# A planned attention and mixture-of-experts kernel: constant products in TensorE's waits, a new order of the first loads, a new list of keys

## The chip, the core and the metric

The kernel runs on one core of one Trainium2 chip. TensorE (PE), VectorE (DVE), ScalarE (ACT), GpSimd (POOL) and SyncE (SP) each work through a queue of their own in program order and meet at semaphores. The metric is the device time of one execution in microseconds, median of three runs: 529.28 us (529.21 to 529.37).

## The reference

Attention over 4 batches of 8 heads (768 positions, head size 64), where a query sees the first 4 keys and the 128 keys up to itself. The result, as 3072 rows of 512, goes to the one of 8 experts whose normalised embedding has the largest dot product with the row, weighted by the softmax over the 8.

```python
scores = scale * q @ k.T
keep = is_sink | in_window
a = exp(where(keep, scores, -1e9) - max); a /= sum
x = (a @ v) as [3072, 512]
logits = (x/|x|) @ (emb/|emb|).T / tau
e = argmax(logits); gate = softmax(logits)[e]
out[rows of e] = gate * (relu(x @ w1[e]) @ w2[e])
```

## The kernel before

The attention works on 16 pairs of heads (`p`), each in 6 blocks of 128 queries (`n = 6 p + j`), in two groups of three blocks. For a block: scores on PE into one of three `sp` buffers (`scores`, L1134), the mask and the maximum on DVE (`merge` L1142 to L1146, `top` L1152), the exponential on ACT (`exp`, L1163), which frees the `sp` buffer. For a group: transposes on PE (L1229), copied out by ACT to `PT` (L1234), cut to the window by POOL to `PA` (L1313 to L1317); the four sink columns go by POOL (`psn`, L1213 to L1219), PE (L1286) and ACT (`pst`, L1291); then the values on PE (`av`, L1328 and L1331), a copy on ACT (`oT`, L1336), and products with the identity and the expert embeddings (`xe`, L1341), whose result `xr` goes to DRAM rows `xs`, and whose logits are summed.

Pairs 0 and 1 are "plain": their keys and queries are used as fp32 from `raw1` and `raw2` (`early_loads` loads them, L1072 scales the queries). Later pairs are split into two fp32r parts: keys `kn` to `kt` by ACT (`k1`, L1096) and POOL (`k2`, L1099), queries `qn` on DVE (L1103, L1107).

After every fourth pair the batch is routed (`route`): argmax on DVE, rank products on PE (L399 to L403), places and one-hots on DVE, `bv` on POOL (L431), the table products on PE (L437), which give `perm`, the list of rows for each expert. The last batch is routed in two halves; there ACT also makes the counts `cnt` (L1407 to L1409), and PE reads the first expert's width from them.

The order on all queues is written by a planner (`Plan.order`): every task has an engine, a duration, a key and dependencies; a simulated clock takes, of the tasks that could start within 0.1 us of the earliest, the one with the lowest key. Keys are block numbers plus the offsets in `KEYS` (for the last pair `LAST`). The SP queue carries most loads; eight DMAs can be under way, so the ninth load waits for the first issued, the tenth for the second.

Then comes one section with its own order (`moe`): POOL gathers the rows of the first expert by `perm`; PE runs three products of 512 columns with constants (L628), reads the widths, and branches (`Switch`) to one of 17 copies ("arms") of an expert's PE code, by width. A hint can announce a branch's target ahead of it; for the first arm `first_width` gives it (L1414), within the attention's plan. In the arm, PE transposes the gathered rows (L646) and runs L691 (first layer) and L730 (second layer).

Of the kernel before, what the change touches and what calls it, by code (L numbers as in the profile page):

```python
# [40 lines left out]
LAST = dict(sel=10.5, ps=35.75, pse=1.25, av=20, ote=-47.25, xe=-20, xee=-8.25, k1=-19, k2=29.25, q1=-74, q2=27.5, sc=4.75, mg=86, tp=-21.5, ex=32.5, sk1=29.75, tr=-21.5, te=64.5, rt=9.75, vs=-1.5, em=23.75, rc=123, lgm=29.75)  # L41
# [3 lines left out]
class Task:  # L45


    def __init__(self, eng, dur, key, fn, deps, use, form):
        self.eng, self.dur, self.key, self.fn, self.deps, self.use, self.form = eng, dur, key, fn, deps, use, form
        self.start = self.end = None  # L50
# [7 lines left out]
class Plan:  # L58
# [7 lines left out]
        "SP": dict.fromkeys(("PE", "ACT", "DVE", "POOL", "SP"), 2.2),  # L66
# [8 lines left out]
    def add(self, eng, dur, key, fn, deps=(), use=(), form=None):  # L75
        t = Task(eng, dur, key, fn, [d for d in deps if d is not None], [b for b in use if b is not None], form)
        for b in t.use:
            b.users.append(t)
        self.tasks.append(t)
        return t  # L80
# [17 lines left out]
    def order(self):  # L98
        todo = {}
        for i, t in enumerate(self.tasks):  # L100
            t.i, t.waits, t.ready, t.next = i, len(t.deps), 0.0, []
# [125 lines left out]
class Kernel:  # L227
# [6 lines left out]
    def constants(self, cp):  # L234
# [8 lines left out]
        raw = self.raw  # L243
        rf = T("rf", [P, 4])
        sv = T("sv", [P, 2])
# [4 lines left out]
        fl = T("fl", [P, 2])  # L250
        nc.vector.tensor_scalar(fl[:, 0:1], sv[:, 0:1], 4.0, None, op0=ALU.is_equal)
        nc.vector.scalar_tensor_tensor(out=fl[:, 1:2], in0=sv[:, 1:2], scalar=128.0, in1=fl[:, 0:1], op0=ALU.is_equal, op1=ALU.mult)
        fi = T("fi", [P, 1], I32)
        nc.vector.tensor_copy(fi[:], fl[:, 1:2])
# [4 lines left out]
        nc.gpsimd.affine_select(out=self.ident[:], in_=one[:], pattern=[[-1, P]], compare_op=ALU.is_equal, fill=0.0, base=0, channel_multiplier=1)  # L259

# [107 lines left out]
    def route(self, b, lg, rp, ps_tile, a=0, m=NB, last=False):  # L368
# [81 lines left out]
        return [("DVE", 1.1, argmax), ("PE", 0.2, rank), ("DVE", 0.4, place), ("DVE", 0.4, index), ("DVE", 0.3, onehot), ("POOL", 0.1 + 0.07 * m, values), ("DVE", 0.07 + 0.134 * m, ranks), ("DVE", 0.3, sums), ("DVE", 0.25, positions), ("PE", 0.4, table), ("DVE", 0.15, gather)]  # L450
# [161 lines left out]
    def head(self, flow):  # L612
# [19 lines left out]

        warm(CAP, 3)
# [407 lines left out]

    def wt(self):
        return self.psw.tile([P, 512], F32, tag="w", name="w")
# [15 lines left out]

    def plain_load(self, p, i, engines=None):  # L1060
# [5 lines left out]
    def prep_plain(self, plan, p):  # L1066
# [5 lines left out]
        t = plan.add("DVE", 0.47, NB * (p - 1) + 1, lambda: self.nc.vector.tensor_scalar(q, q, 0.125, None, op0=ALU.mult), [l], [b])  # L1072
# [43 lines left out]
    def scores(self, n):  # L1116
# [3 lines left out]
        sp = self.pss.tile([P, 2, 512], F32, tag="sp", name="sp")  # L1120
# [121 lines left out]
    def back(self, plan, p):  # L1242
# [128 lines left out]
        if hp == 3:  # L1371
# [8 lines left out]
            for g, (a, m) in enumerate(groups if last else [(0, NB)]):  # L1380
                rt, wb, ts = [], None, []
                for i, (eng, dur, _) in enumerate(self.route(b, None, None, None, a, m)):
# [16 lines left out]
                    if last and g and i == 9:  # L1399
                        plan.add("PE", 0.7, k1 - 50, self.first_width, [t])  # L1400
# [160 lines left out]
```

## Time and profile before

| | |
|---|---|
| median of three runs | 529.28 us |
| the profiled execution | 530.1 us |
| its span | 528.3 us |
| TensorE busy | 492.7 us (93%) |
| attention, to the last `xe` product | 0 to 197 us |
| last routing and start of the experts | 197 to 218.2 us |
| experts | 218.2 to 519 us |

The profiled execution's span leaves out 1.8 us at its ends, and the execution is 0.8 us longer than the median of the three runs. A view by windows gives the busy time of each engine in a stretch; a timeline gives start and length of each piece of work, with what ended the idle time before it in square brackets; the chain of waits is followed back from the last instruction.

### The profile page before, as it was taken

To read this page: it belongs to the slowest core of one execution; us is meant where nothing else is said; L and a number is where in the kernel's file an instruction comes from. 1 tells how busy PE (TensorE), PEld (TensorE's weight loads), DVE (VectorE), ACT (ScalarE), POOL (GpSimd) and SP (SyncE) were. 2 spreads that over 40 slices of the span, in tenths; PEclk is the share of its full clock that TensorE was granted. 3 is DMA by queue.
4 is the path that set the end of the run, shared out by engine and by line. 5 is a ranking of instruction groups with operands and counts; after the bars stand their busy time and mean duration, and the time that the engine had idled before them with its cause. 6 is when DMAs were issued, how large, how long until landed. Compare 5 with 4: busy or idle time off the path is not lost.

```text
span 528.3 us, 9424 instructions
## 1 busy us (share of the span) xinstructions
PE 492.7 (93%) x3338; PEld 414.8 (79%) x3338; DVE 337.5 (64%) x697; ACT 303.1 (57%) x843; POOL 239.6 (45%) x404
## 2 busy tenths in 40 slices
PE   3999999999999984999999999998999999999993
PEld 2577776777766762899999788898998998888982
DVE  4767777678788725796575646496876655562620
ACT  3788886786878741566366345376574653463500
POOL 5668676677687533731540630462706303300311
PEclk9999999999999997899999999999999999999998
DMA  7884553435541122483191561092744704510101
GB/s 254 302 287 135 201 153 113 132 121 155 152 121 35 33 60 73 127 279 122 51 376 45 187 225 40 14 366 104 282 164 146 279 27 149 195 41 2 73 21 48
DMA packets 37356, 75.19 MB, mean 142 GB/s; under 512 B 7032, under 2 KB 19320, under 8 KB 37283
## 3 DMA queue, kind: packets, MB, share of 16 engines
q1 hardware_dynamic: 32018, 58.88, 33.5%
q0 software_dynamic: 5120, 14.95, 8.2%
q8 instruction: 45, 0.74, 0.6%
q10 hardware_dynamic: 144, 0.39, 0.2%
q14 instruction: 29, 0.23, 0.1%
HBM read 61.43 MB, written 14.88 MB: 144 GB/s over the span
## 4 chain that ended last, share of the span: by engine, by line
PE 84%; DVE 6%; DMA 4%; issue 3%; ACT 1%; POOL 1%; SPq 0%; POOLq 0%; DVEq 0%; ACTq 0%
PE b L691 26%; PE b L730 23%; PE sp L1134 7%; PE w L1331 7%; PE w L1341 4%; PE w L1229 4%; PE t L705 2%; PE t L718 2%; PE b L744 2%; PE w L1286 2%; PE w L1328 2%; DMA raw<-in_k_dram 1%; DMA qn<-in_q_dram 1%; PE t L744 1%; DVE mx L1152 1%
## 5 line engine op out<-in xcount | busy, mean ns | idle before, releaser
L730 PE MATMUL b<-hh,W 128*128 128x432 f32 (+6 forms) x448 | 120.2, 344 | 0.0
L691 PE MATMUL b<-xh,W 128*128 128x432 f32 (+7 forms) x512 | 102.7, 343 | 4.3 <-issue 4.3
L691 PEld LDWEIGHTS b<-xh,W 128*128 128x128 f32 x512 | 85.7, 188 | 10.7 <-issue 6.0
L730 PEld LDWEIGHTS b<-hh,W 128*128 128x128 f32 x448 | 79.9, 188 | 4.7
L587 DVE TENSOR_TENSOR W<-raw,W 128x512 fp32r<-128x512 f32 (+1 forms) x96 | 82.2, 870 | 0.3 <-ACT W L585 0.3
L1163 ACT ACTIVATE PM<-sp,mx 128x132 f32<-128x132 f32 (+1 forms) x192 | 69.2, 373 | 13.0 <-DVE mx L1152 11.0
L730 PE MATMUL b<-hl,W 128*128 128x432 f32 (+6 forms) x224 | 75.9, 339 | 0.0
L695 ACT ACTIVATE hh<-b 128x512 fp32r<-128x512 f32 x64 | 38.3, 598 | 63.7 <-PE b L691 63.6
L585 ACT CAST W<-raw 128x512 fp32r<-128x512 f32 (+1 forms) x96 | 71.4, 763 | 4.0 <-SPq L513 4.0
L598 POOL TENSOR_TENSOR gn<-gss,half 128x4 f32<-128x4 f32 x8 | 8.4, 1044 | 137.6 <-ACT gjunk L590 137.6
L696 DVE SCALAR_TENSOR_TENSOR hl<-b,hh 128x512 fp32r<-128x512 f32 x64 | 44.2, 690 | 40.8 <-ACT hh L695 40.6
L555 POOL DMA_INDIRECT out_dram<-ys,perm x32 | 34.2, 1069 | 58.5 <-DVE ys L722 24.4
L691 PE MATMUL b<-xl,W 128*128 128x432 f32 (+7 forms) x256 | 55.6, 338 | 0.0
L1142 DVE COPY_PREDICATED sp<-mask,sp 128x256 f32<-128x256 int32 x80 | 33.4, 425 | 31.0 <-PE sp L1134 21.6
L800 ACT COPY yT<-b 128x512 f32<-128x512 f32 x28 | 16.4, 587 | 57.3 <-PE b L730 57.3
L1134 PE MATMUL sp<-kt,q 64*128 64x260 f32 x504 | 46.8, 305 | 1.1 <-ACT PM L1163 1.1
L1331 PE MATMUL w<-PA,vn 128*64 128x256 f32 (+1 forms) x448 | 46.3, 347 | 0.0
L691 PEld LDWEIGHTS b<-xl,W 128*128 128x128 f32 x256 | 44.0, 188 | 2.5
L730 PEld LDWEIGHTS b<-hl,W 128*128 128x128 f32 x224 | 42.2, 188 | 2.1
L1134 PEld LDWEIGHTS sp<-kt,q 64*128 64x128 f32 x504 | 33.9, 185 | 12.3 <-issue 7.5
L551 POOL DMA_INDIRECT xg<-xs,perm x32 | 33.8, 1057 | 16.1 <-issue 10.0
L1331 PEld LDWEIGHTS w<-PA,vn 128*64 128x64 f32 x448 | 28.7, 139 | 15.7 <-issue 5.9
(193 smaller groups left out, 844.8 us busy)
## 6 DMA issues: line engine op xcount, KB each, us to landing
raw<-in_moe_w_dram SPq DMA_DIRECT2D x64, 512.0 KB, 5.3
vn<-in_v_dram SPq DMA_DIRECT2D x16, 384.0 KB, 3.5
xs<-xr SPq DMA_DIRECT2D x16, 384.0 KB, 3.2
kn<-in_k_dram SPq DMA_DIRECT2D x14, 396.0 KB, 3.7
qn<-in_q_dram SPq DMA_DIRECT2D x14, 384.0 KB, 3.9
raw<-in_k_dram SPq DMA_DIRECT2D x2, 396.0 KB, 5.8
xg<-xs,perm POOLq DMA_INDIRECT x32, 7.4
out_dram<-ys,perm POOLq DMA_INDIRECT x32, 4.8
```

The costliest lines, as they stand in the source:

```text
L551: flow.add("POOL", lambda c=c: self.nc.gpsimd.indirect_dma_start(out=self.xg[e % 2][:, c, :], out_offset=None, in_=self.xs, in_offset=Offs ...
L555: return self.nc.gpsimd.indirect_dma_start(out=self.outv[4 * e + c], out_offset=Offset(ap=perm[:, e, c : c + 1], axis=0), in_=self.ysb[:, ...
L585: flow.add("ACT", lambda: nc.scalar.copy(w[:, 0, c, s], r), keys, [hi])
L587: flow.add(eng, lambda: en.tensor_tensor(out=w[:, 1, c, s], in0=r, in1=w[:, 0, c, s].bitcast(F32), op=ALU.subtract), keys + [hi], [lo])
L691: m = nc.tensor.matmul(h[:, :N], lhsT=W1[:, l, d, fs], rhs=r[:, d, :N], start=j + d == 0, stop=j + d == NDB + 1)
L695: A("ACT", lambda: nc.scalar.activation(hh[:, f, :], h[:], AF.Relu), [hk], [("hh", f)])
L696: A("DVE", lambda: nc.vector.scalar_tensor_tensor(out=hl[:, f, :], in0=h[:], scalar=0.0, in1=hh[:, f, :].bitcast(F32), op0=ALU.max, op1=AL ...
L730: m = nc.tensor.matmul(y[:, :N], lhsT=W2[:, l, f, ms], rhs=r[:, f, :N], start=f + j == 0, stop=f + j == NFB + 1)
L1134: nc.tensor.matmul(sp[:, h, : KW + P], lhsT=q[hs[h], js], rhs=k[hs[h], ks], start=i == 0, stop=i == len(parts) - 1)
L1142: nc.vector.copy_predicated(sp[:, :, 0:P], self.mask[:], sp[:, :, KW : KW + P])
L1163: self.nc.scalar.activation(PM[:, c, h, 0 : hi - lo], sp[:, h, lo:hi], AF.Exp, bias=mx[:, h : h + 1], scale=1.0, accum_out=self.SM[b][:, j ...
L1331: nc.tensor.matmul(o[0][64 * h : 64 * h + 64, (q - a) * P : (q - a + n) * P], lhsT=vt[0][:, h, j, :], rhs=PA[g][0][:, j - lo + 1, h, q - j ...
```

## The change

Four things change. First, `early_loads` issues pair 0's keys ahead of everything on SP; the three small loads follow, then pair 1. Second, products of the constant `one` (128x128) are put on PE: 12 at the start, 8 behind the third score block, and in the last routing 6 and 6 behind the two halves' rank products and 4 behind the last table product. Third, the announcement of the first arm moves from the attention's plan into the section. Fourth, durations, the DMA's delay (2.2 to 3.0), earliest starts (`at`) and all keys of the planner are new, and expert 0's weight loads may not be placed before 100 us of the planner's clock. Computed is the same.

```diff
+FILL = {(0, 1): 6, (1, 1): 6, (1, 9): 4}
-KEYS = dict(form=2, sel=-24.5, ps=1.5, pse=-1.5, av=3.5, ote=-61.25, xe=12.25, xee=2.25, k1=-6.25, k2=-75.75, q1=-0.25, q2=-122.25, sc=-0.25, mg=-2.25, tp=-6.5, ex=-0.5, sk1=112.5, tr=-55.75, te=-86.25, rt=-3.5, vs=3.25, em=6.25, rc=48, lgm=33.25)
+KEYS = dict(form=14.5, sel=146, ps=0.5, pse=-39, av=-1, ote=-56.25, xe=15.25, xee=2.75, k1=-5.75, k2=-139.75, q1=15.75, q2=-217.25, sc=9.25, mg=-4.75, tp=-28, ex=-3, sk1=125, tr=-72.25, te=-138.75, rt=-1.5, vs=1.25, em=-0.75, rc=130, lgm=80.25)
...
-        "SP": dict.fromkeys(("PE", "ACT", "DVE", "POOL", "SP"), 2.2),
+        "SP": dict.fromkeys(("PE", "ACT", "DVE", "POOL", "SP"), 3.0),
...
+        A("PE", lambda: nc.switch_hint(engines=[nc.tensor], index=[self.width[0]], n=NW + 1, label="expert0") and None)
         warm(CAP, 3)
...
+    def warm(self, plan, n, dur, key, deps=(), at=0.0, kind="w"):
+        wb = plan.buf(kind)
+
+        def f():
+            w = self.wt() if kind == "w" else self.score_tile()[:, 0, :]
+            for _ in range(n):
+                self.nc.tensor.matmul(w[:, 0:P], lhsT=self.one[:], rhs=self.one[:], start=True, stop=True)
+
+        plan.add("PE", dur, key, f, deps, [wb], None, at)
...
+                if n == 2:
+                    self.warm(plan, 8, 1.72, n + K["sc"] + 0.1, [t])
...
+                    if last and (g, i) in FILL:
+                        self.warm(plan, FILL[g, i], 0.215 * FILL[g, i], k1 - 45 + i, ts[-1:], 0.0, "sp")
...
     def first_width(self):
-        PE = mybir.EngineType.PE
         self.width = self.width_of(0, 1)
-        self.tc.switch_hint({PE: self.width[0]}, NW + 1, "expert0")
...
-            t = plan.add(eng, dur, KEYS["vs"] + 0.5 * i, fn, [t])
+            t = plan.add(eng, dur, KEYS["vs"] + 0.5 * i, fn, [t], at=0.0 if i else 8.0)
         self.vs_task = t
+        self.warm(plan, 12, 4.6, -1000, at=1.4)
+        plan.add("DVE", 1.1, 2 * NB, self.plain_case, at=6.0)
...
-            t = plan.add(eng, dur, KEYS["em"] + 0.3 * i, fn, [t], [wb] if i in (3, 4) else [])
+            t = plan.add(eng, dur, KEYS["em"] + 0.3 * i, fn, [t], [wb] if i in (3, 4) else [], at=0.0 if i else 7.0)
...
-                plan.add("SP", 1.5, NB * 12, lambda raw=raw, src=src, n=n, i=i: self.load_w(raw, src, n, (i,)), (), [b])
+                plan.add("SP", 1.3, NB * 14, lambda raw=raw, src=src, n=n, i=i: self.load_w(raw, src, n, (i,)), (), [b], at=100.0)
...
-        nc.sync.dma_start(self.raw[:], self.ints.bitcast(I32).partition_broadcast(P))
-        for i, eng in ((0, nc.vector), (1, nc.gpsimd))[: len(PLAIN)]:
+        def small():
+            nc.sync.dma_start(self.raw[:], self.ints.bitcast(I32).partition_broadcast(P))
+            nc.sync.dma_start(self.em[:], self.emb)
+            nc.sync.dma_start(self.tau_t[:], self.tau.partition_broadcast(P))
+
+        for i, eng in ((0, nc.vector), (1, nc.gpsimd)):
             k, _ = self.plain_views(i)
             eng.memset(k[:, 0:P], 0.0)
-            if PLAIN[i] == i:
-                self.plain_load(i, i, (nc.sync, (nc.scalar, nc.sync)[i]))
...
+            self.plain_load(i, i, (nc.sync, (nc.scalar, nc.sync)[i]))
+            if i == 0:
+                small()
```

What the planner makes of it is seen in the queues. The start of ACT's queue before; `kt_166<-kn` is pair 2's key split, `IE,ess<-em` the squares of the expert embeddings, `vh<-vraw` the sink values, `PM,sums<-sp,mx` the exponentials of pair 0:

```order
L1063 DMA raw_65<-in_q_dram 128x768
L1492 ACT_TABLE_LOAD
L1492 ACTIVATE first_exp<-first_exp 1x1
L340 ACTIVATE IE,ess<-em 8x512
L1013 CAST vh<-vraw 32x1024
L1163 ACTIVATE PM,sums<-sp,mx 128x128 x2
L1163 ACTIVATE PM,sums<-sp,mx 128x132 x2
L1096 CAST kt_166<-kn 128x792
L1163 ACTIVATE PM,sums<-sp,mx 128x132 x2
L1019 ACTIVATE vs<-vraw,hmask 32x16x64
```

And the same place in the changed kernel:

```order
L1080 DMA raw_65<-in_q_dram 128x768
L1517 ACT_TABLE_LOAD
L1517 ACTIVATE first_exp<-first_exp 1x1
L1113 CAST kt_160<-kn 128x792
L343 ACTIVATE IE,ess<-em 8x512
L1017 CAST vh<-vraw 32x1024
L1180 ACTIVATE PM,sums<-sp,mx 128x128 x2
L1180 ACTIVATE PM,sums<-sp,mx 128x132 x4
L1023 ACTIVATE vs<-vraw,hmask 32x16x64
```

The key split of pair 2 has moved from behind the second block's exponentials to the head of the queue, ahead of the squares, the sink values and every exponential. The start of PE's queue before (`raw_65` and `raw_66` are pairs 0 and 1):

```order
L1134 MATMUL sp<-raw_65 128x260 x10
L1229 MATMUL w<-ident,PM 128x128 x6
L1134 MATMUL sp<-raw_65 128x260 x2
L358 MATMUL w<-ident,em 128x8 x4
L1134 MATMUL sp<-raw_66 128x260 x2
L1286 MATMUL w<-ident,psn 32x128 x3
L1134 MATMUL sp<-raw_66 128x260 x2
L1328 MATMUL w<-pst,vs 128x384
```

And in the changed kernel:

```order
L1073 MATMUL w<-one 128x128 x12
L1151 MATMUL sp<-raw_65 128x260 x6
L1073 MATMUL w<-one 128x128 x8
L1151 MATMUL sp<-raw_65 128x260 x4
L1248 MATMUL w<-ident,PM 128x128 x6
L1151 MATMUL sp<-raw_65 128x260 x2
L1305 MATMUL w<-ident,psn 32x128 x3
L361 MATMUL w<-ident,em 128x8 x4
L1151 MATMUL sp<-raw_66 128x260 x4
L1248 MATMUL w<-ident,PM 128x128 x6
L1151 MATMUL sp<-raw_66 128x260 x2
L1347 MATMUL w<-pst,vs 128x384
```

Constant products stand ahead of the first block and behind the third; the values of the first group (L1347) come one group of six transposes and one score block later than before. Last, the end of PE's attention work, before:

```order
L1331 MATMUL w<-PA,vn 64x256 x4
L1331 MATMUL w<-PA,vn 64x128 x2
L1341 MATMUL w<-IE,oT 128x144 x6
L399 LDWEIGHTS tri_b
L399 MATMUL w<-oh_3092,tri_b 128x24
```

And in the changed kernel:

```order
L1360 MATMUL w<-IE,oT 128x144 x3
L1347 MATMUL w<-pst,vs 128x384
L1350 MATMUL w<-PA,vn 64x128 x2
L1350 MATMUL w<-PA,vn 64x256 x4
L1350 MATMUL w<-PA,vn 64x128 x2
L1360 MATMUL w<-IE,oT 128x144 x3
L402 LDWEIGHTS tri_b
L402 MATMUL w<-oh_3108,tri_b 128x24
```

The first half's `xe` products now come ahead of the second half's values, and the second half's follow their own values with no other product between.

## Rows read from the trace of the kernel before

**Rows 1.** The head of the page.

```profile
span 528.3 us, 9424 instructions
```

**Rows 2.** Windows by stage: stretch and its length, then busy time and count of PE, PEld, DVE, ACT and POOL, granted clock, DMA share, GB/s.

```profile
0.00:25.00 25.00, 15.68 (x65) 9.03 (x65) 15.22 (x46) 13.99 (x43) 16.34 (x60) 1.00 0.79 272
25.00:197.00 172.00, 168.14 (x1494) 121.67 (x1490) 123.64 (x318) 131.55 (x505) 116.49 (x241) 1.00 0.43 134
197.00:218.20 21.20, 12.28 (x52) 8.28 (x51) 12.84 (x43) 4.67 (x10) 7.86 (x9) 0.76 0.32 85
218.20:519.00 300.80, 296.53 (x1733) 275.85 (x1732) 185.02 (x291) 152.83 (x287) 97.89 (x94) 1.00 0.41 144
```

**Rows 3.** Timeline of TensorE in the first 36 us: start, length, line, tile, shape, count.

```profile
7.15 2.97 PE L1134 MATMUL sp<-raw 64*128 64x260 f32 x12 [7.15 <-DVE fi L254]
...
14.05 1.54 PE L1229 MATMUL w<-ident,PM 128*128 128x128 f32 x6
...
21.22 2.40 PE L1331 MATMUL w<-PA,vn 128*64 128x256 f32 x12
...
25.25 0.55 PE L1229 MATMUL w<-ident,PM 128*128 128x128 f32 x3
...
34.80 1.30 PE L1331 MATMUL w<-PA,vn 128*64 128x256 f32 x12
```

**Rows 4.** Timeline of the SP queue (SPq) and ACT in the first 24 us.

```profile
0.80 0.39 SPq L1480 DMA_DIRECT2D raw<-in_ints_dram  x1
...
6.45 0.43 SPq L1086 DMA_DIRECT2D kn<-in_k_dram  x1
...
8.91 0.63 ACT L340 ACTIVATE IE<-em 8x512 f32<-8x512 f32 x1 [6.18 <-DMA em<-in_moe_expert_emb_dram]
...
10.23 1.04 ACT L1013 CAST vh<-vraw 32x1024 fp32r<-32x1024 f32 x1 [0.59 <-DMA vraw<-in_v_dram]
...
11.18 0.35 ACT L1163 ACTIVATE PM<-sp,mx 128x128 f32<-128x128 f32 x1
...
12.80 0.85 ACT L1096 CAST kt<-kn 128x792 fp32r<-128x792 f32 x1
...
13.55 0.36 ACT L1163 ACTIVATE PM<-sp,mx 128x132 f32<-128x132 f32 x1
...
14.26 1.13 ACT L1019 ACTIVATE vs<-vraw,hmask 32x1024 fp32r<-32x1024 f32 x1
...
23.67 0.48 ACT L1336 COPY oT<-w 128x384 f32<-128x384 f32 x1 [1.50 <-PE w L1331]
```

**Rows 5.** DMA issues, each asked for by the window of its issue (at 0.81, 1.24, 6.45 and 15.62 us): what, queue, count, size, us from issue to landing.

```profile
raw<-in_q_dram ACTq DMA_DIRECT2D x1, 384.0 KB, 5.2
...
raw<-in_k_dram SPq DMA_DIRECT2D x1, 396.0 KB, 5.8
...
kn<-in_k_dram SPq DMA_DIRECT2D x1, 396.0 KB, 6.3
...
kn<-in_k_dram SPq DMA_DIRECT2D x1, 396.0 KB, 3.7
```

**Rows 6.** Who TensorE waited for between 25 and 197 us: line, releaser, us in total, times, longest.

```profile
PE sp L1134 <- ACT PM L1163: 1.1, 1, 1.1
PE w L1286 <- DVE rk L407: 0.6, 1, 0.6
PE w L437 <- POOL bv L431: 0.6, 1, 0.6
...
PE w L437 <- DVE eo L453: 0.4, 2, 0.2
```

**Rows 7.** Timeline of the last routing.

```profile
195.48 0.48 ACT L1336 COPY oT<-w 128x384 f32<-128x384 f32 x1 [1.34 <-PE w L1331]
196.40 0.25 DVE L1267 TENSOR_TENSOR lgp<-w,lr 128x48 f32<-128x48 f32 x1 [5.88 <-PE w L1341]
...
198.51 0.18 DVE L385 TENSOR_TENSOR oh<-wdesc,m1l 128x24 bf16<-128x24 f32 x1
...
201.84 0.18 DVE L407 TENSOR_TENSOR rk<-w,oh 128x24 f32<-128x24 f32 x1 [0.59 <-ACT cnt L1409]
...
204.06 0.82 PE L437 MATMUL w<-bv,av 128*128 128x32 f32 x3 [0.22 <-DVE pacc L440]
...
204.92 0.19 DVE L440 TENSOR_TENSOR perm<-w,pacc 128x32 int32<-128x32 f32 x1 [0.86 <-PE w L437]
```

**Rows 8.** Windows around the start of the experts; the columns are those of rows 2.

```profile
202.00:203.00 1.00, 0.00 (x0) 0.00 (x0) 0.93 (x6) 0.00 (x0) 0.00 (x0) 0.69 0.00 0
206.00:209.00 3.00, 2.88 (x4) 1.34 (x5) 2.08 (x3) 0.85 (x1) 1.97 (x2) 0.50 0.14 20
...
213.00:216.00 3.00, 3.00 (x12) 2.52 (x11) 2.27 (x4) 1.11 (x2) 0.93 (x1) 0.50 0.27 87
```

**Rows 9.** The chain of waits at the first arm (start, length, what); what TensorE waited for at the first layer of the experts behind it, from 200 us on (us in total, times, longest); and the instruction queue between 210.0 and 210.2 us (fetches, MB, share).

```profile
211.23 1.39 issue
212.62 1.11 PE b L646 x4
...
PE b L691 <- issue: 4.3, 4, 1.6
...
q8 instruction: 1, 0.02, 31.2%
```

More of the change, by code (lines that the diff above doesn't have):

```diff
@@ L73, in buf, with add @@
         return Buf(kind)
-    def add(self, eng, dur, key, fn, deps=(), use=(), form=None):
-        t = Task(eng, dur, key, fn, [d for d in deps if d is not None], [b for b in use if b is not None], form)
+    def add(self, eng, dur, key, fn, deps=(), use=(), form=None, at=0.0):
+        t = Task(eng, dur, key, fn, [d for d in deps if d is not None], [b for b in use if b is not None], form, at)
         for b in t.use:
@@ L100, in order @@
         for i, t in enumerate(self.tasks):
-            t.i, t.waits, t.ready, t.next = i, len(t.deps), 0.0, []
+            t.i, t.waits, t.ready, t.next = i, len(t.deps), t.at, []
             todo.setdefault(t.eng, []).append(t)
@@ L240, in T, with plain_case @@
             return t
-        raw = self.raw
-        rf = T("rf", [P, 4])
-        sv = T("sv", [P, 2])
+        T("rf", [P, 4])
+        T("sv", [P, 2])
+        T("fl", [P, 2])
+        T("fi", [P, 1], I32)
+        one = T("one", [P, P])
+        nc.gpsimd.memset(one[:], 1.0)
+        T("ident", [P, P])
+        nc.gpsimd.affine_select(out=self.ident[:], in_=one[:], pattern=[[-1, P]], compare_op=ALU.is_equal, fill=0.0, base=0, channel_multiplier=1)
+    def plain_case(self):
+        nc, raw, rf, sv, fl, fi = self.nc, self.raw, self.rf, self.sv, self.fl, self.fi
         nc.vector.tensor_copy(rf[:], raw[:])
@@ L448, in positions @@
             self.positions(b, a, m, st["m1"], st["pos"], T("eo", [P, m]))
-        return [("DVE", 1.1, argmax), ("PE", 0.2, rank), ("DVE", 0.4, place), ("DVE", 0.4, index), ("DVE", 0.3, onehot), ("POOL", 0.1 + 0.07 * m, values), ("DVE", 0.07 + 0.134 * m, ranks), ("DVE", 0.3, sums), ("DVE", 0.25, positions), ("PE", 0.4, table), ("DVE", 0.15, gather)]
+        return [("DVE", 1.1, argmax), ("PE", 0.2, rank), ("DVE", 0.4, place), ("DVE", 0.4, index), ("DVE", 0.3, onehot), ("POOL", 0.1 + 0.07 * m, values), ("DVE", 0.07 + 0.134 * m, ranks), ("DVE", 0.3, sums), ("DVE", 0.25, positions), ("PE", 0.6, table), ("DVE", 0.15, gather)]
     def positions(self, b, a, m, m1, pos, eo):
@@ L1071, in prep_plain @@
         l = None if PLAIN.index(p) == p else plan.add("SP", 2.2, NB * p - 9, lambda: self.plain_load(p, i), (), [b])
-        t = plan.add("DVE", 0.47, NB * (p - 1) + 1, lambda: self.nc.vector.tensor_scalar(q, q, 0.125, None, op0=ALU.mult), [l], [b])
+        t = plan.add("DVE", 0.47, NB * (p - 1) + 1, lambda: self.nc.vector.tensor_scalar(q, q, 0.125, None, op0=ALU.mult), [l], [b], at=(5.5, 7.5)[i])
         self.Q[p] = [(None, None, [t], [b])]
@@ L1204, in front @@
                 t = plan.add("PE", 0.45 if p in PLAIN else 0.351, n + K["sc"], lambda n=n: self.scores(n), deps, [sb] + qb, "sc")
-                t = plan.add("DVE", 0.34 if n % NB != 1 else 0.46, n + K["mg"], lambda n=n: self.merge(n), [t], [sb])
+                if n == 2:
+                    self.warm(plan, 8, 1.72, n + K["sc"] + 0.1, [t])
+                t = plan.add("DVE", 0.34 if n % NB != 1 else 0.53, n + K["mg"], lambda n=n: self.merge(n), [t], [sb])
                 mb = plan.buf("mx")
@@ L1348, in xee @@
                 (nc.scalar.copy if act else nc.vector.tensor_copy)(xr[0][:, a : a + m, :], w[0])
-            t = plan.add("PE", sum(0.418 if n == 2 else 0.206 for _, _, n in mm) + 0.3, kg + K["av"], av, [sel_t, pe[g], lv, self.vs_task], [b_pst, b_pa[g], bv, ob, b_oT], "av")
+            t = plan.add("PE", sum(0.418 if n == 2 else 0.206 for _, _, n in mm) + 0.42, kg + K["av"], av, [sel_t, pe[g], lv, self.vs_task], [b_pst, b_pa[g], bv, ob, b_oT], "av")
             t = plan.add("ACT", 0.1 + 0.09 * m, kg + K["ote"], ote, [t], [ob, b_oT])
-            t = plan.add("PE", 0.245 * m, kg + K["xe"], xe, [t, self.ie_task], [b_oT, wb, b_xr], "tr")
+            t = plan.add("PE", 0.26 * m, kg + K["xe"], xe, [t, self.ie_task], [b_oT, wb, b_xr], "tr")
             if last:
```

24 lines of the change are left out of this document (9 added, 15 removed).

## The prediction

> **What bounds the kernel now.** I read the windows by stage first. TensorE is busy 168.1 of the 172 us from 25 to 197 and 296.5 of the 300.8 us of the experts [rows 2]; in both stages a delay ahead of them is passed on whole, and little can be won inside them. Two stretches have room: the first 25 us, where PE is busy 15.7, and the 21.2 us from the last attention product to the first expert layer, where it is busy 12.3 at a mean granted clock of 0.76 [rows 2]. The expert stage's code is the same but for the announcement.
>
> The second view is PE's timeline of the first us. The clock column reads 1.00 for the first 25 us [rows 2], but the products say otherwise: twelve value products took 2.40 us at 21.2 and 1.30 at 34.8, six transposes 1.54 at 14.05 and three 0.55 at 25.25 [rows 3]. So PE ran near half speed, the level of 1.2 GHz, until about 24.5, and the column simply holds no earlier change. Half of PE's work up to there is what a high clock could save, if PE is what the others wait for.
>
> The third view, ACT's timeline, asks that. ACT waits for the embeddings until 8.91 and the sink values until 10.23, then does two blocks' exponentials from 11.18, pair 2's key split at 12.80, the third block at 13.55, and is free of the first group at 14.26 [rows 4]. The key split ran as `kn` landed: issued 6.45, 6.3 us to land, 12.75 [rows 4, 5].
>
> **The change part by part.** Durations are those of the profiled execution, 530.1 us with a span of 528.3 [rows 1]; it was 0.8 us longer than the median of the three runs, 529.28. By its own time the sum below gives 531.7; I put it on the median.
>
> *The first us.* The 12 constant products cost nothing: PE has nothing else until 7.15 [rows 3]. Pair 0's keys are now SP's first issue, at 0.80 instead of the integers [rows 4], and should land 5.2 to 5.8 us later [rows 5], at 6.0 to 6.6, so the first scores start some 0.5 us earlier and, with a raised clock, three blocks take about half of 2.97 us [rows 3]. The 8 products behind them cover a wait. None of this is on the path, because of what happened to ACT's queue. The key split of pair 2 now stands at its head, ahead of squares, sink values and all exponentials. ACT works in order, so all these wait for `kn`. Its issue waits, as tenth load, for the landing of pair 0's keys: 6.0 to 6.6, about where it was (6.45). With the same loads ahead of it I take 6.0 us to landing: 12.4. Then the split (0.75 to the next start, from 12.80 to 13.55), the squares (0.63 and the reading of their sum, some 0.75), the sink values (0.95, from 10.23 to 11.18) [rows 4]: the first exponential at about 14.85, not 11.18. Three blocks at 0.7 to 0.8 end at 17.05, not 14.26: +2.8 us, with the split no longer to do.
>
> Is that made up by a faster PE? From the fourth block on PE needs `sp` buffers that the exponentials free. It has then stood since about 9.6 (scores from 6.6 for 1.5, eight products for 1.5, at a third of the 0.55 that three transposes of the same shape took at full speed [rows 3]) until 15.6, 6 us. In the last routing the clock was at the lower level some 5 us after the attention's last products at 197, small rank products in between [rows 2, 8]. So I expect it to be low again when work resumes, and to rise, as before, only with the first values; the stretch from 14.05 to 24.5 is repeated, later. I take +2.8.
>
> The bounds: `kn` lands at best 3.7 us after its issue, as a later load did [rows 5], at 9.7; the shift is then about 0. If the clock is held as well, the ten us of PE work up to 24.4 shrink by up to half, but ACT, which waited for PE only 1.5 us in its longest case there [rows 4], then sets the pace: I allow −3. At the other end the clock rises one group of values later, and 2 us more of work run at half speed: +4.8.
>
> A page of the Trainium skill speaks against the 12.4: "DMA: Bandwidth & Descriptors", section "Anatomy of one DMA", gives an unshared transfer as about 2.0 us and its bytes at 436 GB/s, by my estimate 2.9 us for 396 KB. By that `kn` would be there at about 9.2 and the stage would not be late. Behind seven other loads the row shows 6.3, and alone 3.7, so the trace agrees with neither half of it here.
>
> *The weight loads* of expert 0 leave the first 35 us for a stretch near 100 us. Their data is first used behind 205 us, so I cost the move at 0; were they late, ACT's first weight split would wait for them.
>
> *The middle.* Of PE's waits from 25 to 197, 1.6 us lie at the routings of earlier batches (0.6, 0.6, 0.4) and 1.1 at one score block [rows 6]. In the new order the products between a batch's rank and table products are 2.5 to 4 times as many (27, 21 and 21 before, 76, 52 and 91 now), so the table no longer waits. I take −1.0; bounds −2.5 (nearly all waits gone) and +1.5 (new ones as large as the old elsewhere).
>
> *The end of attention.* The first half's routing steps on DVE, 196.40 to 198.69 [rows 7], can now run beside the second half's values. But the second half's `xe` products follow directly on ACT's copy of those values, 0.48 us and two hand-overs [rows 7], with PE idle, and the six transposes of the last group stand close behind the last scores. I take +1.0 for these waits and −0.7 for the shorter chain (the place of the second half still waits for ACT's counts, as at 201.84): +0.3; bounds −0.8 and +1.1. The two fills of 6 lie in waits and cost nothing. The last fill stands ahead of the section, which every engine enters on all others: four products at 0.2 to 0.4 us behind the table, against a `perm` that is ready 0.2 us behind it, less what a higher clock takes off the last table product (half of 0.82 [rows 7]): +0.3; bounds −0.4 and +1.0.
>
> *The first arm.* POOL's gather ends the chain at 211.23, and PE enters the arm 1.39 us later; the instruction queue fetches at 210.0 [rows 9] and not at all between 195 and 210, though the announcement stands ahead of the table products. Announced in the section, ahead of three products, the fetch can come early. The seven later arms, announced likewise in the arm before, lost 4.3 us in four of them [rows 9], 0.6 on the mean; so I take 0.6 − 1.39 = −0.8, bounds −1.4 and +0.2. "Runtime: NRT & Kernel Launch" in the Trainium skill, section "Instruction fetch mechanics", says that a taken branch outside the two fetched pages must fetch before it goes on; by it the whole 1.39 goes once the page is announced in time, and the row on later arms says that often it does not. I expect the transposes behind, at 0.50 from 213 to 216 [rows 8], to stay slow: the three constant products end sooner at a high clock, and the gather lets PE stand as before.
>
> Sum: 2.8 − 1.0 + 0.3 + 0.3 − 0.8 = +1.6, and 529.28 + 1.6 = 530.9 us. About 0.2% (1.06 us) is what a measurement of this kernel can tell from no change.
>
> **The rivals.**
>
> *The load is early and the clock is held.* `kn` at about 9.7 us puts the first exponential at 12.2; PE stands some 3 us only, keeps the high level, and runs the first two pairs at full speed: −2.5 for the first us. From there all else as above: −2.5 − 1.0 + 0.6 − 0.8 = −3.7, 525.6 us. For it: 3.7 us for a lone load [rows 5]. Against it: seven loads ahead of `kn`, and 5.2 to 6.3 us for every early one. Chance 0.18. The rest gives −1.2, so it decides for faster once this stage costs less than about +0.1.
>
> *ACT is late, but the new list pays for it.* All routing waits and the one on scores go (−2.5) and the arm is entered at once (−1.4): 2.8 − 2.5 + 0.6 − 1.4 = −0.5, 528.8 us. For it: the many more products between rank and table. Against it: PE is at 168 of 172 already. Chance 0.22.
>
> *The announcements and fills do nothing.* The arm is entered as late as before, the last fill holds up the section by its full length (+0.6): 2.8 − 1.0 + 0.3 + 0.6 = +2.7, 532.0 us. For it: later arms that wait in spite of an announcement [rows 9]. Chance 0.15.
>
> **How the numbers follow.** The forecast has 0.45; its own range is 529.6 to 532.8. Of it I put 0.34 beyond +1.06, 0.08 within, 0.03 below −1.06. The first rival is faster (0.18). The second is spread about no change: 0.10 faster, 0.10 within, 0.02 slower. The third is slower, 0.12, else within. Faster 0.31, within 0.21, slower 0.48. For 8 in 10 the range takes in the later rise of the clock at the top, 533.4, and most of the first rival at the bottom, 526.8.
>
> **What would show it.** In the profile after: ACT's first piece behind the table load is the key split, ended by the landing of `kn` at 12 to 13 us, and the first exponential stands at 14 to 16. Fourth score block near 15.6, six transposes at about 1.5 us, first values near 24 to 28 at about 2.4 us. PE's waits between 25 and 197 hold no table product; PE waits for ACT's copy ahead of its last products. An instruction fetch between 206 and 209, and less than 1.4 us ahead of the first arm. I am wrong if `kn` lands before 10.5 us, if the value products of the first group run at 1.3 us, or if attention ends before 197 although ACT was late.

## The result, and the profile after

The changed kernel took 533.69 us (median of 8 runs, 531.3 to 536.12), beside 529.25 for the kernel before on the same chip: a ratio of 1.009, with an interval of 1.0064 to 1.0116. It is slower, as forecast, but by about 4.8 us (by the ratio) instead of 1.6, and just above the range. Both kernels spread by several us from run to run; later runs of the kernel before lay between 525.2 and 532.9, with medians of 527.3 to 528.6. Two slow executions of it, 560.5 and 695.1 us, are left out of every comparison. So experiments are compared by their ratio to the kernel before on their own chip; 0.1% is 0.53 us.

The profiled execution of the changed kernel has a span of 533.0 us against 528.3 [rows 1]. Windows by stage, as in [rows 2], the third up to the first layer of the experts, the last around one place of the middle:

```profile
0.00:25.00 25.00, 17.21 (x98) 13.05 (x98) 12.97 (x41) 12.45 (x38) 13.95 (x60) 0.86 0.63 218
25.00:197.00 172.00, 165.43 (x1474) 120.91 (x1474) 130.84 (x322) 133.04 (x509) 117.07 (x242) 0.99 0.46 141
197.00:222.40 25.40, 18.20 (x111) 13.99 (x110) 13.51 (x43) 5.13 (x11) 8.78 (x9) 0.87 0.29 76
222.40:523.00 300.60, 295.93 (x1732) 275.69 (x1731) 185.81 (x291) 152.80 (x287) 96.14 (x93) 1.00 0.41 144
135.00:140.00 5.00, 3.77 (x20) 3.07 (x20) 4.90 (x15) 3.15 (x14) 1.31 (x5) 0.66 0.20 73
```

TensorE is busy 165.4 of the 172 us from 25 to 197, where it was 168.1, and the granted clock falls once inside this stage, at 136 us. From the first layer to the end the experts take 310.6 us, where they took 310.1.

The first us, on TensorE and then on ACT (start, length, line, tile; answers to [rows 3, 4]):

```profile
8.10 2.05 PE L1073 MATMUL w<-one 128*128 128x128 f32 x16
16.40 2.11 PE L1151 MATMUL sp<-raw 64*128 64x260 f32 x8 [6.25 <-ACT PM L1180]
18.44 1.54 PE L1248 MATMUL w<-ident,PM 128*128 128x128 f32 x6
24.97 1.30 PE L1350 MATMUL w<-PA,vn 128*64 128x256 f32 x12
...
13.24 0.85 ACT L1113 CAST kt<-kn 128x792 fp32r<-128x792 f32 x1 [10.50 <-DMA kn<-in_k_dram]
15.56 0.35 ACT L1180 ACTIVATE PM<-sp,mx 128x128 f32<-128x128 f32 x1
```

ACT is late as forecast, 15.56 instead of 14.85, since `kn` took 7.4 us to land. TensorE stands 6.25 us and the six transposes are slow, as forecast. But the first values run at 1.30, at the high clock.

What TensorE waited for from 25 to 201 us (us in total, times, longest; answers to [rows 6]):

```profile
PE w L1248 <- DVE xr L1367: 4.4, 2, 2.3
PE w L1248 <- ACT oT L1355: 0.9, 2, 0.5
PE w L1360 <- ACT oT L1355: 0.8, 2, 0.6
PE w L1248 <- ACT PM L1180: 0.4, 1, 0.4
PE sp L1151 <- ACT PM L1180: 0.3, 1, 0.3
```

The waits of the rank and table products are gone. In their place stand two for one and the same thing, DVE's copy of `xr`, 2.1 and 2.3 us long. The second of them in the timeline, with what ran on POOL and DVE ahead of it:

```profile
131.76 1.87 POOL L1116 TENSOR_TENSOR kt<-kn,kt 128x792 fp32r<-128x792 f32 x1
131.79 1.86 DVE L420 TENSOR_TENSOR ch<-ch,rm 128x6 f32<-128x6 f32 x1
133.91 0.35 DVE L426 TENSOR_TENSOR bs<-slot_f,ch 128x192 f32<-128x192 f32 x1
135.58 0.59 DVE L1367 COPY xr<-w 128x432 f32<-128x432 f32 x1
136.23 0.90 PE L1248 MATMUL w<-ident,PM 128*128 128x128 f32 x3 [2.28 <-DVE xr L1367]
```

A DVE instruction on six elements per partition takes 1.86 us; in the last routing the same line takes 0.16. It begins with POOL's key split and ends with it. The transposes behind the wait take 0.90 instead of 0.55: the clock has fallen.

The chain of waits around the first arm (start, length, what; answers to [rows 9]):

```profile
207.16 1.00 PE sp L1073 x8
208.76 1.01 issue
209.76 3.80 DMA xg<-xs,perm
213.59 0.70 DVE xg L571
214.29 1.38 issue
215.68 1.11 PE b L650 x4
```

The last four constant products are in the chain, and the issue ahead of the arm is 1.38 us, as it was. By the ends or starts of five steps, before and after: end of the first half's values 193.61 and 195.97 (from 192.31 and 194.67, 1.30 each), end of `perm` 205.11 and 207.38, POOL's gather 206.73 and 209.76, the arm 212.62 and 215.68, the first layer 218.21 and 222.43. The lag is 2.4, 2.3, 3.0, 3.1 and 4.2 us, and 4.7 at the end.

### The profile page after: what moved, and what is told of

Read it like the earlier page. It is cut to its first block, busy times and chain, and to the rows that moved or that the text cites. A ratio compares the mean times of both kernels' runs of the same rounds, so it can differ in the third digit from the quotient of the medians.

```text
span 533.0 us, 9579 instructions
## 1 busy us (share of the span) xinstructions
PE 497.6 (93%) x3410; PEld 424.0 (80%) x3410; DVE 343.9 (65%) x697; ACT 303.4 (57%) x843; POOL 236.9 (44%) x404
## 4 chain that ended last, share of the span: by engine, by line
PE 83%; DVE 6%; issue 3%; DMA 3%; ACT 3%; POOLq 0%; POOL 0%; SPq 0%; ACTq 0%; DVEq 0%
PE b L695 26%; PE b L734 22%; PE sp L1151 7%; PE w L1350 6%; PE w L1248 5%; PE w L1360 4%; PE t L709 2%; PE t L722 2%; PE b L748 2%; PE w L1347 2%; ACT PM L1180 2%; PE w L1305 2%; DMA kn<-in_k_dram 1%; DVE sp L1159 1%; PE t L748 1%
## 5 line engine op out<-in xcount | busy, mean ns | idle before, releaser
L590 DVE TENSOR_TENSOR W<-raw,W 128x512 fp32r<-128x512 f32 (+1 forms) x96 | 85.4, 904 | 0.3 <-ACT W L588 0.3
L804 ACT COPY yT<-b 128x512 f32<-128x512 f32 x28 | 16.4, 587 | 57.4 <-PE b L734 57.4
L1159 DVE COPY_PREDICATED sp<-mask,sp 128x256 f32<-128x256 int32 x80 | 33.3, 423 | 23.2 <-PE sp L1151 16.4
L1350 PE MATMUL w<-PA,vn 128*64 128x256 f32 (+1 forms) x448 | 45.2, 341 | 0.0
L1151 PEld LDWEIGHTS sp<-kt,q 64*128 64x128 f32 x504 | 34.2, 186 | 11.4 <-issue 5.8
L554 POOL DMA_INDIRECT xg<-xs,perm x32 | 32.6, 1020 | 17.0 <-issue 10.5
```

What stands on the lines that cost most here:

```text
L554: flow.add("POOL", lambda c=c: self.nc.gpsimd.indirect_dma_start(out=self.xg[e % 2][:, c, :], out_offset=None, in_=self.xs, in_offset=Offs ...
L590: flow.add(eng, lambda: en.tensor_tensor(out=w[:, 1, c, s], in0=r, in1=w[:, 0, c, s].bitcast(F32), op=ALU.subtract), keys + [hi], [lo])
L1151: nc.tensor.matmul(sp[:, h, : KW + P], lhsT=q[hs[h], js], rhs=k[hs[h], ks], start=i == 0, stop=i == len(parts) - 1)
L1159: nc.vector.copy_predicated(sp[:, :, 0:P], self.mask[:], sp[:, :, KW : KW + P])
L1350: nc.tensor.matmul(o[0][64 * h : 64 * h + 64, (q - a) * P : (q - a + n) * P], lhsT=vt[0][:, h, j, :], rhs=PA[g][0][:, j - lo + 1, h, q - j ...
```

## The experiments

**One kernel without the start products, one with ACT's split moved back.** The first:

```diff
-            for _ in range(n):
+            for _ in range(0 if n in (12, 8) else n):
```

> The changed kernel without its 20 constant products in the first us (12 ahead of the first block, 8 behind the third); all else stands in the same order. Theory 1 (the products raise the clock before the first block, and that paid for ACT's late start): the first blocks, transposes and values run at half speed again until about 25 us, 4 to 5 us of work twice as long, so the time rises by 3 to 5 us, to about 537.5, and the first values take 2.4 us instead of 1.30. Theory 2, the prediction's (the products do nothing, ACT and the stand behind the third block set the stage): 533.7 within 1 us, and the first values take 1.30 or 2.40 as they did.

Measured: 533.95 us, ratio 1.0098 (1.0061 to 1.0135). That is no change from the changed kernel's 1.009. The first values still run fast, and begin half a us earlier:

```profile
16.02 2.10 PE L1151 MATMUL sp<-raw 64*128 64x260 f32 x8 [6.95 <-ACT PM L1180]
18.05 1.37 PE L1248 MATMUL w<-ident,PM 128*128 128x128 f32 x6
24.48 1.30 PE L1350 MATMUL w<-PA,vn 128*64 128x256 f32 x12
```

So the first theory fell: the products did not pay for anything. The clock rose behind the work that starts at 16 us, late but without gaps, with or without products ahead of it. The second kernel moves two tasks in the planner's finished order (`KS[0]` are pair 2's splits, `X[0][2]` the third block's exponentials; this is the body of the function that does it):

```diff
...
+    for t in self.KS[0]:
+        order.remove(t)
+    i = order.index(self.X[0][2]) + 1
+    return order[:i] + list(self.KS[0]) + order[i:]
...
```

> The changed kernel with pair 2's two key splits (ACT's and POOL's) put behind the third block's exponentials; no other instruction is moved. Theory 1 (ACT's wait for pair 2's keys is the loss of the first us, and holding the clock up is worth as much): the first exponential stands at 11.2 to 11.6 instead of 15.56, TensorE's stand of 6.25 us shrinks to about 2 us, the clock isn't lowered there, and the time falls by 3 to 5 us, to 529 to 530.5. Theory 2 (the embeddings, sink values or the next keys end the first stage anyway, or a later wait takes the gain): less than 1 us, 533 to 533.7.

Measured: 532.98 us, ratio 1.008 (1.0051 to 1.0109), within 0.1% of the changed kernel. The exponentials do begin at 12.28, but the gain is not kept:

```profile
10.00:14.00 4.00, 1.39 (x11) 0.80 (x11) 1.91 (x4) 2.67 (x11) 0.00 (x0) 1.00 1.01 358
14.00:17.50 3.50, 3.47 (x14) 1.76 (x13) 2.79 (x8) 2.98 (x8) 2.21 (x2) 0.51 1.04 399
17.50:21.00 3.50, 2.13 (x15) 1.13 (x15) 3.27 (x8) 2.69 (x14) 3.21 (x7) 0.99 0.66 194
21.00:27.70 6.70, 6.70 (x30) 3.80 (x30) 5.39 (x11) 4.80 (x14) 4.31 (x7) 0.50 0.15 55
```

TensorE now starts earlier, with gaps, and the granted clock is at half for 3.5 us and, after a stretch with 1.4 us idle, for 6.7 us more, in which TensorE is busy throughout.

**POOL's split in quarters.** Same order on every queue; the one subtraction of 792 columns becomes four of 198.

```diff
-            nc.gpsimd.tensor_tensor(out=kb, in0=kf(), in1=ka.bitcast(F32), op=ALU.subtract)
+            for s in (slice(c, c + NB * KW // 4) for c in range(0, NB * KW, NB * KW // 4)):
+                nc.gpsimd.tensor_tensor(out=kb[:, s], in0=kf()[:, s], in1=ka[:, s].bitcast(F32), op=ALU.subtract)
```

> The changed kernel with POOL's part of each key split issued as four quarter-width subtractions instead of one of 1.87 us; every queue keeps its order. Theory 1 (DVE's instructions whose operands all lie in SBUF stand still while POOL's subtraction runs, 27.16 and 131.79 us in the trace, DVE's copy of xr then comes late and TensorE stands 2.1 and 2.3 us): DVE waits for a quarter at most, no DVE instruction there takes over 1.2 us, both waits of TensorE fall under 1 us, the clock stays up at 136 us, and the time falls by 2.5 to 4.5 us, to about 530. Theory 2 (DVE is late because of its own order, POOL only happens to run): the waits stay at about 2 us, 533.7 or, with POOL's extra issue, up to 534.5.

Measured: 527.52 us, ratio 0.9994 (0.9972 to 1.0015): 0.96% less than the changed kernel, about 5.1 us, more than the first theory had. By the two intervals the difference is uncertain by some 1.8 us. The same place in the trace, and the first half's last values, which stood at 194.67:

```profile
130.77 3.13 POOL L1117 TENSOR_TENSOR kt<-kn,kt 128x198 fp32r<-128x198 f32 x4
130.80 0.60 DVE L420 TENSOR_TENSOR ch<-ch,rm 128x6 f32<-128x6 f32 x1
133.36 0.59 DVE L1367 COPY xr<-w 128x432 f32<-128x432 f32 x1
...
190.17 1.30 PE L1350 MATMUL w<-PA,vn 128*64 128x256 f32 x12
...
PE w L1248 <- DVE xr L1367: 2.2, 2, 1.2
...
135.00:140.00 5.00, 4.37 (x38) 3.52 (x36) 4.90 (x14) 3.65 (x17) 3.04 (x5) 1.00 0.43 127
```

DVE is held for one quarter, 0.60 us, and then goes between the quarters. The waits for `xr` halve to 2.2 us, the longer one to 1.2, not under 1 us each as the theory had it, and the clock stays up at 136. The first half's values come 4.5 us earlier, so nearly the whole gain lies ahead of them. The quarters cost POOL more (0.73 each on the mean, 39.0 us in all against 26.2), and that costs nothing. DVE's own order as the cause is excluded: it is the same. The fall of the clock goes with the whole splits: in all five profiles that have them with the new list it falls between 135 and 141 us, and in none of the eight of this list with quarters, for all pairs or for 3 and 12, does it fall between 30 and 195.

With quarters for pairs 3 and 12 alone:

```diff
-            for s in (slice(c, c + NB * KW // 4) for c in range(0, NB * KW, NB * KW // 4)):
+            for s in (slice(c, c + NB * KW // m) for m in (4 if p in (3, 12) else 1,) for c in range(0, NB * KW, NB * KW // m)):
```

> The changed kernel with POOL's key split in four quarters for pairs 3 and 12 alone, whose splits stood at 26.64 and 131.76 us; the other twelve splits stay whole. Theory 1 (of all splits only these two hold DVE where TensorE waits for it): nearly the whole gain of the run with all splits in quarters (527.5), 527.3 to 529. Theory 2 (the gain is the sum of many small ones): at most half of it, 530.5 to 532.5.

Measured: 529.17 us, ratio 1.0023 (0.9993 to 1.0053), 0.67% of the 0.96%. By the medians two of the fourteen splits make some two thirds of the loss, but the spread (0.3 to 0.4% on each) leaves anything from some third to all of it. The first theory is nearly right, the second is not.

The quarters in the kernel before, by the same two lines as above:

> The kernel before with every one of POOL's key splits in four quarters; nothing else. Theory 1 (the old list puts the splits where DVE's hold-ups, 8 us of them, do not reach TensorE, whose waits between 25 and 197 us come to 3.9 us): 0 to 1.5 us less than before. Theory 2 (quarters help any list, so that the loss is not the new list's): 4 to 6 us less, 523 to 525.

Measured: 526.12 us, ratio 0.9975 (0.9946 to 1.0005), about 1.3 us less, at the edge of the spread. The old list had such collisions too, by my estimate 8 us of DVE's time if each instruction is set against its like, where the new list has some 13, but TensorE hardly waited for them. So by the medians some 3.8 of the 5.1 us are the new list's. With quarters in both kernels the change costs 0.19%, 1.0 us, which is within the spread. This trace shows one thing more. The queues of the first us are those of the kernel before, apart from the quarters, yet:

```profile
11.71 2.10 PE L1134 MATMUL sp<-raw 64*128 64x260 f32 x8 [1.60 <-ACT PM L1163]
13.75 1.54 PE L1229 MATMUL w<-ident,PM 128*128 128x128 f32 x6
19.29 1.30 PE L1331 MATMUL w<-PA,vn 128*64 128x256 f32 x12
...
0.00:16.20 16.20, 7.46 (x30) 4.64 (x30) 9.00 (x30) 8.35 (x24) 10.33 (x53) 1.00 0.77 279
16.20:25.00 8.80, 7.51 (x54) 4.26 (x53) 8.13 (x20) 7.43 (x28) 7.21 (x16) 1.00 0.81 264
```

Here the products run fast from about 16.2 us and the first values take 1.30 at 19.29, where the profile of before had 2.40 at 21.22 [rows 3]. A third trace of this order, that of the best of both below, has the clock up from about 16.7 us, at half from 20.1 to 23.5, and 2.40 for these values at 20.66.

**The old list with the rest of the change** (products at the same places, the first loads and the announcement as after; the cut shows where the products are put in):

```diff
...
+        self.fill(12)
         for t in plan.order():
             t.fn()
+            self.fill(getattr(t, "fill", 0))
...
```

> The kernel before, its list and its order, with the constant products at the same places (12, 8, 6, 6, 4), pair 0's keys loaded first and the announcement in the section: the change without its new list. Theory 1 (the loss is the new list's; the products and the announcement are worth nothing, the last four cost 0.8): 528.5 to 530, within 1 us of before. Theory 2 (products or loads carry a part of the loss): 531 or more; if the products at the start are worth something where ACT is not late: 526 to 527.5.

Measured: 529.9 us, ratio 1.0035 (1.0004 to 1.0066), 1.8 us slower than before: in the expected band of times, though not within 1 us of its own comparison. Of these, 0.77 us are the last four products (from `perm` to the gather 2.38 against 1.61); the exponentials start at 12.46 instead of 11.18, behind sink values that are loaded later. The new list makes the difference to 1.009, 0.55% or 2.9 us, uncertain by some 2 us.

**The last routing.** Without the 6, 6 and 4 products:

```diff
-            for _ in range(n):
+            for _ in range(0 if n in (6, 4) else n):
```

> The changed kernel without the 6, 6 and 4 constant products in the last routing; all else in the same order. Theory 1 (they hold the clock up there, which gives about 1.5 us, and the last four hold up the section by 0.76 us): from the end of the attention's last products to perm 7 to 8 us instead of 6.4, from perm to POOL's gather 1.6 instead of 2.4, and the arm's transposes run slow for longer or as long; the time is 0.5 to 1.5 us higher, about 534.7. Theory 2 (they do nothing but delay the section): 0.8 us lower, 532.9.

Measured: 533.08 us, ratio 1.008 (1.0045 to 1.0115). From the last `xe` product to `perm` 6.70 us instead of 6.38, from `perm` to the gather 1.61 instead of 2.38. The sixteen products together are worth 0.32 us and cost 0.77; the second theory stands in the main, though the times alone (1.008 and 1.009) do not separate the two kernels. Without the last four alone (`n in (4,)`), with quarters:

> The changed kernel with all splits in quarters and without the last four constant products ahead of the section. Theory 1 (these four hold up every engine's entry): from perm to POOL's gather 1.61 us instead of 2.37, and the time 0.8 us under that of the run with quarters alone (527.5), 526.7. Theory 2 (they keep the clock up behind them, and without them the arm's transposes run slow for longer): the entry is earlier, but the stretch from the arm to the first layer grows from 4.70 to 5.5 us or more, and the time is 527.5 or higher.

Measured: 526.52 us, ratio 0.9984 (0.9955 to 1.0013), 0.1% under the quarters alone; the gather comes 1.62 us behind `perm`, and it took 4.43 us from the arm to the first layer, not longer. The trace is that of theory 1; the times do not separate them.

On that kernel, pair 2's split moved back by the lines above; and, in another, the 20 start products taken out (`n in (4, 12, 8)`):

> The changed kernel with all splits in quarters and without the last four constant products (526.5 alone), and in addition pair 2's key splits behind the third block's exponentials. Theory 1 (ACT's late start costs what the prediction said, 2.8 us, and the spread of the earlier run hid it): 523 to 524.5. Theory 2 (TensorE's clock takes back what an earlier start gives): 525.5 to 527, with a stretch at half clock between 14 and 28 us that is longer than without the move.

> The changed kernel with all splits in quarters, without the last four and without the 20 constant products of the first us. Theory 1 (the start products change nothing, as the earlier run without them had it): 526 to 527.2, as with them (526.5). Theory 2 (their worth was hidden by the spread): 528 or more.

Measured: 528.23 us, 1.0005 (0.9977 to 1.0033), and 527.49 us, 0.9992 (0.9969 to 1.0014). Against 0.9984 neither is a gain; the first is above what either theory had, the second between its two. The first had TensorE at half clock from 12.8 to 16.3 and from 19.7 to 29.9 us, longer than without the move, as theory 2 had it. Taking back ACT's late start does not win time here.

**The best of both.** The kernel before, quarters, and the first half's `xe` products ahead of the second half's values, by a move in the planner's finished order:

```diff
...
+    (_, to, xe), (av, _, _) = self.tail[-2:]
...
+    order.remove(xe)
...
+    i = order.index(av)
+    return order[:i] + ([to] if to not in order else []) + [xe] + order[i:]
...
```

> The kernel before with its own list, all splits in quarters, and one move of the new order's tail: the first half's xe products ahead of the second half's values. Theory 1 (TensorE's added waits for ACT's copies, some 0.8 us, are paid for by the first half's routing beside the second half's values): 0.3 to 1 us less than the quarters alone (526.1), 525.1 to 525.8. Theory 2 (the two cancel): 526 to 526.5.

Measured: 526.99 us, 0.9995 (0.9972 to 1.0018), not better than the quarters alone (0.9975). In the trace the move costs: from the end of the first half's values to the last `xe` product it is 4.98 us instead of 3.49, with two waits of 0.58 for ACT's copies, and from there to `perm` only 0.4 less. No kernel here is faster than the one before beyond doubt; the nearest are the two at 526.1 and 526.5.

**The announcement.** Left out of the changed kernel:

```diff
-        A("PE", lambda: nc.switch_hint(engines=[nc.tensor], index=[self.width[0]], n=NW + 1, label="expert0") and None)
```

> The changed kernel without any announcement of the first arm. Theory 1 (the announcement is without effect at either place): TensorE enters the arm 1.3 to 1.6 us behind the gathered rows, as with it (1.39), and the time is that of the changed kernel, 532 to 535. Theory 2 (it works in the section, and the 1.39 us are something else's): the gap grows by 0.6 us or more.

Measured: 534.16 us (two runs, 1.0123, 1.0067 to 1.0179), and 1.38 us from the gathered rows to the arm, as with it. It did nothing. But in one kernel, the one with quarters and without the last four and the start products, the arm came at once:

```profile
204.96 0.96 POOL L554 DMA_INDIRECT xg<-xs,perm  x1 [0.30 <-issue]
207.37 0.69 DVE L571 TENSOR_TENSOR xg<-xg 128x512 f32<-128x512 f32 x1 [2.42 <-DMA xg<-xs,perm]
208.12 0.66 PE L650 MATMUL b<-ident,xg 128*128 128x128 f32 x4 [0.32 <-DVE xg L571]
...
q8 instruction: 1, 0.02, 2.7%
```

The last row is the instruction queue from 203.4 to 206 us: one fetch, which the same window of the kernel with start products does not have. Three variants of it: that line left out, the announcement back in `first_width`, and the 12 start products kept (`n in (4, 8)`):

> The kernel with quarters and without the last four and the 20 start products, in which TensorE entered the first arm 0.32 us behind the gathered rows where all others took 1.35 to 1.71, and here without the announcement. Theory 1 (there the announcement worked, and in the other kernels something hides it): the gap goes back to 1.3 to 1.7 us, and the instruction fetch ahead of the arm comes some 2.5 us before it instead of 3.7. Theory 2 (the announcement never works; where the code lies decides): the gap stays under 0.5 us.

> The same kernel with the announcement at its old place, ahead of the last table products instead of in the section. Theory 1 (the place decides): a gap of 1.3 to 1.7 us, as in the kernel before. Theory 2 (the place is indifferent, where the code lies decides): under 0.5 us, as in the section.

> The changed kernel with quarters, without the last four and without the 8 products behind the third block, but with the 12 at the start: the announcement in the section as in the changed kernel, the code of TensorE in between by length. Theory 1 (a page's end near the section hides the announcement, and the length of the code ahead decides): either gap is possible, and a gap under 0.5 us goes with an instruction fetch between the section's entry and the gathered rows. Theory 2 (the 12 products themselves hide it): 1.3 to 1.7 us.

Measured from the end of DVE's `xg` to the arm: 1.43 us without the announcement, 0.06 with it at the old place, 0.06 with it in the section, and 1.71 with the 12 start products back. (One run each: 527.84, 525.49 and 526.69 us, too few to compare times.) So the announcement works at either place in the kernel without those products, and in no other one here. Whether the products themselves or the length of TensorE's code ahead decides, these runs don't show. It gains little even there. From the gathered rows to the first layer that kernel took 5.68 us, and the one in which the announcement failed and the clock was up 5.85, for its chain of waits does not pass the arm's entry:

```profile
207.77 4.24 DMA xg<-xs,perm
212.04 0.70 DVE xg L571
212.78 0.66 PE b L650 x4
213.44 0.86 PE t L631 x4
```

The copy of the fourth gather ends at 212.74 here, where TensorE entered the arm at 209.68, and at 212.35 in the kernel that entered it at 208.12, whose gathers began 0.27 us earlier.

## Why the prediction was wrong

The direction held, the size did not, and the direction held in part by luck: the +2.8 us on which "slower" rested measured +0.6, and 2.7 us of the loss came from collisions that no term of the sum had. By the steps of the sum, all from one profiled execution each:

**The first us, +2.8; between the two profiles +0.6.** The same work, nine score blocks, two groups of transposes and the first group's values, lies ahead of these products before, after, and in the kernel before with quarters:

```profile
25.64 0.49 PE L1286 MATMUL w<-ident,psn 128*32 128x128 f32 x3
26.20 0.50 PE L1305 MATMUL w<-ident,psn 128*32 128x128 f32 x3
22.94 0.49 PE L1286 MATMUL w<-ident,psn 128*32 128x128 f32 x3
```

The step that failed here is "to rise, as before, only with the first values": the clock rose at 20.1, ahead of them, and the values at 1.30 are one of the prediction's own signs of being wrong. The forecast of ACT's queue, of the stand and of the clock's fall was right to 0.8 us. Behind it lies a worse fault: the stretch from 14 to 24.5 us was taken for a property of the queue, and is one of an execution. In the trace of before with quarters the same order was 2.7 us earlier at this point. Against that one, the changed kernel is 3.3 us late, and +2.8 would have been about right; moving the split back, however, gained nothing. The page "TensorE: Matmul & The Clock Gate" of the Trainium skill, section "The HAM clock gate", says that the number of slow products at a start differs from run to run of one kernel; these traces agree. The fit that gives the prediction's 2.9 us for `kn` is stated in the Trainium skill, "DMA: Bandwidth & Descriptors", section "Anatomy of one DMA", for transfers that GpSimd issues; `kn` is issued by SP, and took 6.3 and 7.4 us.

**The weight loads, 0: 0.** ACT's first weight split begins 0.92 us ahead of POOL's first gather in both profiles.

**The middle, −1.0; from there to the end of the first half's values +1.8.** This is the step that decides. What it says of the table came true, those waits went, and by these traces their size was right: with quarters in both kernels this stretch takes 165.3 us in the new list and 166.3 in the old. (A second trace of the old list with quarters has 167.8, with the clock at half once, near 85 us.) But it counted only the waits that the new list removes, and put what it may bring at 1.5 at most "elsewhere", without a mechanism. With whole splits the stretch takes 169.8 us in the new list and 168.0 in the old, so the collisions cost 4.4 us in the new list and 1.7 in the old, 2.7 more. The mechanism stood in the trace of before, here a query split beside POOL's key split, whose like takes 0.55:

```profile
49.51 1.87 POOL L1099 TENSOR_TENSOR kt<-kn,kt 128x792 fp32r<-128x792 f32 x1
49.88 1.92 DVE L1103 TENSOR_SCALAR q<-qn 128x768 fp32r<-128x768 f32 x1
```

The list decides which DVE instruction meets a key split, and the new one put the split of pair 12 on a batch's routing and that of pair 3 on DVE's query split ahead of an `xr` copy. TensorE then waited 4.4 us for DVE, and after the longer wait its clock fell for 3.4 us. The quarters, which change nothing but the length of the hold, take 5.1 us off. "SBUF — State Buffer" in the Trainium skill, section "SBUF: two separate sides", says that VectorE and GpSimd share one pair of ports, which the first of two instructions that need it holds to its end. The traces agree: L420 was held for 1.86 us by a whole split and 0.60 by a quarter, while instructions that read PSUM, such as the mask at 45.28 with 0.43, kept their time beside a split. I had not asked of this change which of the two would meet.

**The end of attention, +0.3: −0.1** (from the first half's values to `perm`, 11.5 us before and 11.4 after). Right within its bounds, with the help of the fills, which the kernel without them shows to be worth 0.3 of it.

**The last fill, +0.3: +0.77 behind `perm`**, as three other kernels confirm, two without it (1.61 and 1.62 us from `perm` to the gather) and one of the old list with it (2.38). What the higher clock takes off the last table product, 0.51 us instead of 0.82, lies ahead of `perm`, in the term above; taken together the size was about right.

**The first arm, −0.8: 0.0.** The step that failed is that the fetch comes early once the branch is announced in the section: it came at 213.0 to 213.5, not between 206 and 209. Where the announcement did work, it saved 1.4 us at the entry, and the fourth gather took nearly all of it. That the transposes stay slow was right, but they stayed so for 2.4 us more; the way from the arm to the first layer took 6.75 us instead of 5.59, +1.2. In the other kernels it took 4.4 to 6.8, as the low clock fell on it or ahead of it, so this term changes with the run.

Together 0.6 + 1.8 − 0.1 + 0.8 + 0.0 + 1.2 and 0.5 in the experts make, but for rounding, the 4.7 us between the spans. Of the rivals, the one that gave the products and announcements no effect was right on the start products and the announcement, and would have come to 532.0; none had the collision.

## What to carry to other kernels

When a list or planner reorders work, ask not only which waits go but which instructions of VectorE and GpSimd now run at one time: an instruction whose length in the trace is many times that of its like is a wait that no wait view names. A long GpSimd instruction in four parts costs more on GpSimd (here half as much again) and frees VectorE between them. And a profile of the first us is one draw: read a second execution before building on its clock.

## What the runs showed of the hardware that I had not expected

- VectorE's hold by GpSimd is shown as the instruction's own duration (1.86 us for 128x6 elements), not as idle time with a releaser.
- With an unchanged order, the clock of the first us rose at 24.5 us in one execution, near 16.2 in another, and in a third it rose before 17, fell at 20.1 and rose again at 23.5.
- In one execution each: work begun early, with gaps (from 13 to 21 us), was followed by half clock up to 27.7; the same work begun at 16.4, without gaps at first, had the full clock from 20.1.
- An announced branch was entered 0.06 us after its data in the two kernels that lacked the start products and the last four, and 1.35 to 1.71 us after it in the others.
